# P4 of the second layer by a second Strassen level, with the sums of A22 added up by DMAs

## The chip, the core and the metric

The kernel runs on one core of a Trainium2 chip. The metric is the device time of one execution in microseconds; of several runs, the median. Five engines work side by side, each through its own list of instructions in order: TensorE (PE in the profile; its weight loads are PEld), VectorE (DVE), ScalarE (ACT), GpSimd (POOL) and SyncE (SP). SP and POOL also issue DMA transfers, which 16 DMA engines carry out. An instruction that waits for a semaphore holds up everything behind it in its engine's list.

## The reference

A light convolution, then two matrix products with a gate between them:

```python
# x: (8, 4096, 192), weight: (8, 7); softmax over the 7 taps of each of 8 heads
out = einsum('hk,bskhg->bshg', softmax(weight), windows_of_7(x))   # causal
x = out.reshape(32768, 192)
h = x @ w_in                      # 192 x 2048
g = h * clip(h + 3, 0, 6) / 6     # hardswish
return g @ w_out                  # 2048 x 192
```

## The kernel before

The 32768 tokens are taken in 32 blocks of 1024, and each of these as two halves of 512 (N). Block 0 is computed plainly, with `direct_chunk`; blocks 1 to 31 go through `first_layer` and then `second_layer`. The convolution of a later block runs beside them, as VectorE instructions over 128x1536 (L806, "taps").

**First layer.** 16 units, each 18 matmuls of 512 columns into one of four PSUM slots (two banks each). ScalarE computes the relu (L306) and VectorE the gate (L310), which frees the slot. Units 0 to 7 read `y_own` and give the tiles A11 and A22 of g, eight chunks of 128x512 each; units 8 to 15 read `y_other` and give A21 and A12. Beside them POOL forms the small sums of A11 (`small_sums` into `s1`, one pair of chunks after every second unit), then S3 = A11 - A21 (`g_sums(…, (3,), …)`, a pair of chunks after units 9, 11 and 13, the last pair on VectorE) and S1 = A21 + A22. The first two pairs of S1 are adding DMAs issued by POOL (L470, after units 9 and 11), the other two are VectorE adds.

**Second layer.** Written in Winograd's form of Strassen: seven products P1 to P7 of A and B tiles (and of the sums S and T) in place of eight (`prod` names operands of each). A product has 96 output rows, in three column groups q of 32; TensorE is split into four column strips of 32, and strips 0 to 2 compute the column groups of P4, P7, P2, P6, P3. Strip 3 computes P1 and P5, two of whose three column groups are done by one more Strassen level (`level_two`: products 1 to 7 of half size, `small`, on 256 tokens each; the third column group is plain). P1's surplus chunks go to strips 0 to 2.

The order is written out: `put(j, cost, fn)` appends a matmul to the list of strip j and moves its clock on, by 2 for 512 columns and by 1 for 256; one unit of this clock is called a step. `do(t, fn)` puts a copy, a sum or a DMA at time t. At the end all are sorted by time and issued, so a matmul that waits holds up all four strips. The clock sets the order alone; an engine starts an instruction when its own list and its waits allow it. The streams are 82 steps long. P1 to P7 are put together by matmul accumulation in PSUM banks a to e and x_, by ScalarE copies between banks and VectorE adds. `finish` adds and stores the last of a block in the first layer of the next one. SP issues `swap` (y_own to y_other), the loads of x and the stores.

Buffers that matter: `y_own` (two tiles, high and low part of the next block's y), `s1` (shares its tag with the result tiles, so it waits for their stores), A22, which the small sums of P5 (`s5`) overwrite once P4 has been computed.

Of the kernel before, what the change touches and what calls it, by code (L numbers as in the profile page):

```python
# [31 lines left out]
def kernel(  # L32
# [36 lines left out]
    ys = ctx.enter_context(tc.tile_pool(name="ys", bufs=1))  # L69
    ot = ctx.enter_context(tc.tile_pool(name="ot", bufs=1))  # L70
# [50 lines left out]
    y_own = [cst.tile([P, K3, N], F32, name=f"y{n}") for n in range(2)]  # L121
# [4 lines left out]
    w_s = cst.tile([P, 2, 4, NP // 2, QS], F32, name="w_s")  # L126

# [314 lines left out]

    def first_layer(i, jobs):
# [11 lines left out]
        count = 2 * NP  # L455
        for job in jobs.get(-1, ()):
            job()
        for n in range(count):
            unit(n)
            for job in jobs.get(n, ()):  # L460
                job()
# [4 lines left out]
            if n > NP and n % 2:  # L466
                pair = slice(n - NP - 1, n - NP + 1)
                g_sums(nc.gpsimd if n + 1 < count else nc.vector, (3,), range(NP)[pair], 2)
                if n + 3 < count:
                    nc.gpsimd.dma_start(out=S1[:, pair], in_=A22[:, pair], accum_op=ALU.add)  # L470
        for pair in (slice(NP - 2, NP), slice(NP - 4, NP - 2)):
            add(S1[:, pair], A21[:, pair], A22[:, pair])

# [19 lines left out]
    def small_weights(to, w):  # L493
# [5 lines left out]
        for o, p, q in ((t1, b12, b11), (t2, b22, t1), (t3, b22, b12), (t4, b21, t2)):  # L499
            nc.gpsimd.tensor_tensor(out=o, in0=p, in1=q, op=ALU.subtract)  # L500

    def second_layer(i, between):
        last = i + 1 == NB
        ours = [free_slots.pop(0) for _ in range(3)]
        d, e, b, x_, a, c = (psum[:, 2 * n + k] for n in ours for k in range(2))
        ends = [psum[:, 2 * free_slots[0] + k] for k in range(2)] if last else [b, b]
# [5 lines left out]
        B, C, V = (bank[rows(3)] for bank in (x_, d, b))  # L512
        A, E = e[rows(3)], a[rows(3)]
# [28 lines left out]
        def small(n, m_, out, start=False):  # L542

            x, w = prod[n]
            sums, ws = (s1[-1], w_s[:, 0]) if n == 1 else (s5, w_s[:, 1])
            x11, x12, x21, x22 = four_parts(x)
            z1, z2, z3, z4 = four_parts(sums)
# [3 lines left out]
            t1, t2, t3, t4 = (ws[:, k] for k in range(4))  # L551
# [4 lines left out]
            for u in range(NP // 2):  # L556
                put(3, 1, lambda u=u: matmul(
                    3, out[:, lo], wm[:, u], xm[:, u], start and u == 0
                ))
# [14 lines left out]

        for q in range(NQ):
            plain(q, d, 4, q, every, True)
            before = (1, 6, NP)[q]
            plain(q, c, 7, q, every[:before], True)
            plain(q, e, 1, 2, range(5 + q, 6 + q))
            do(clock[q], copy, out=e[rows(q + 1)] if q < 2 else p1[third], in_=e[rows(q)])  # L580
            plain(q, c, 7, q, every[before:])
            plain(q, a, 2, q, every[:6], True)
# [8 lines left out]
        def level_two(n, p, chunks, order):  # L591
# [25 lines left out]
            for step in order.split():  # L617
                if step[0] == "x":
                    fill(int(step[1]))
                elif step[0] in "lh":  # L620
# [326 lines left out]
```

## Time and profile before

| | |
|---|---|
| median of 3 runs | 2220.78 us (2220.66 to 2221.22) |
| the profiled execution | 2220.6 us, its span 2218.5 us |
| granted TensorE clock | 1.0 |
| TensorE busy | 2211.4 us, 100% of the span |
| VectorE busy | 1808.9 us, 82% |
| ScalarE busy | 935.8 us, 42% |
| GpSimd busy | 827.9 us, 37% |
| relu L306 of one unit | 1118 ns, 512 times |
| gate L310 of one unit | 1218 ns, 512 times |
| adding DMA g<-g, 512 KB | 62 times, 5.0 us from issue to landing |

In a line of a timeline stand the start in us from the beginning of the span, the duration in us, the engine, the line of the kernel, the operation, what it writes and reads, how many instructions are merged in it, and in brackets how long the engine had stood idle before it and what ended that. In a line of the chain in order of time stand start, length and what. A group's line has its busy time in us and the mean of one in ns. A matmul of fp32 data is two records in the profile.

### The profile page before, as it was taken

What the parts mean: (1) busy time and instruction counts of PE and PEld (TensorE: products, weight loads), DVE (VectorE), ACT (ScalarE), POOL (GpSimd) and SP (SyncE); (2) the same over time, 40 slices, a digit from 0 to 9 for tenths busy, and PEclk for the clock granted to TensorE, in tenths of its full rate; (3) what the DMA queues carried; (4) which work ended last, traced back from release to release, by engine and by line L of the source; (5) the groups of instructions that cost most, each with busy time, mean ns of one, the idle gap of its engine ahead of it and who ended that gap; (6) DMA issues with size and microseconds to landing.
All of it is one profiled execution on the core that took longest, in us unless ns stands there. A gap on an engine that the chain in (4) does not pass through costs nothing.

```text
span 2218.5 us, 49343 instructions
## 1 busy us (share of the span) xinstructions
PE 2211.4 (100%) x21598; PEld 1535.2 (69%) x21598; DVE 1808.9 (82%) x1588; ACT 935.8 (42%) x1172; POOL 827.9 (37%) x706
## 2 busy tenths in 40 slices
PE   9999999999999999999999999999999999999999
PEld 5567776677776677766777667776667776677766
DVE  8878788888888888888888888888888888888866
ACT  7434443344433444433444334443344433344433
POOL 4434442244422344323444224442244432344322
PEclk9999999999999999999999999999999999999999
DMA  7333323433223332243332333322433224333232
GB/s 165 65 71 69 66 37 67 77 63 77 35 58 78 70 70 49 44 77 70 70 62 40 68 74 66 77 35 59 77 68 73 43 49 77 70 70 57 40 59 34
DMA packets 249095, 142.91 MB, mean 64 GB/s; under 512 B 207120, under 2 KB 212240, under 8 KB 248880
## 3 DMA queue, kind: packets, MB, share of 16 engines
q1 hardware_dynamic: 230392, 105.86, 23.7%
q0 software_dynamic: 17248, 33.64, 8.8%
q8 instruction: 169, 2.77, 0.5%
q10 hardware_dynamic: 1240, 0.27, 0.1%
q14 instruction: 46, 0.38, 0.1%
HBM read 31.72 MB, written 25.17 MB: 26 GB/s over the span
## 4 chain that ended last, share of the span: by engine, by line
PE 99%; ACT 0%; DVE 0%; POOL 0%; DMA 0%; issue 0%; POOLq 0%; ACTq 0%; DVEq 0%
PE psum L528 50%; PE psum L432 47%; PE psum L321 2%; PE psum L730 0%; PE psum L738 0%; ACT g L306 0%; DMA y_other<-y 0%; POOL w_in L220 0%; ACT scale L196 0%; ACT sig L193 0%; ACT sig L199 0%; POOL sig L210 0%; ACT w_in L218 0%; DVE y L283 0%; POOLq L942 0%
## 5 line engine op out<-in xcount | busy, mean ns | idle before, releaser
L528 PE MATMUL psum<-g,w_out 128*32 128x512 f32 (+1 forms) x6712 | 967.4, 552 | 0.0
L306 ACT ACTIVATE g<-psum,half 128x1024 f32<-128x1024 f32 x512 | 572.3, 1118 | 494.0 <-PE psum L432 465.8
L310 DVE SCALAR_TENSOR_TENSOR g<-g,psum 128x1024 f32<-128x1024 f32 x512 | 618.8, 1218 | 195.1 <-ACT g L306 194.8
L491 POOL TENSOR_TENSOR s<-g 128x256 f32<-128x256 f32 x248 | 268.8, 1084 | 1252.5 <-DVE g L310 915.9
L528 PEld LDWEIGHTS psum<-g,w_out 128*32 128x32 f32 x6712 | 370.8, 110 | 246.9 <-issue 126.7
L432 PE MATMUL psum<-y,w_in 64*128 64x512 f32 x4608 | 534.8, 388 | 0.3
L432 PE MATMUL psum<-y_other,w_in 64*128 64x512 f32 x4608 | 529.0, 386 | 0.1
L432 PEld LDWEIGHTS psum<-y,w_in 64*128 64x128 f32 x4608 | 428.6, 184 | 121.3 <-issue 26.0
L432 PEld LDWEIGHTS psum<-y_other,w_in 64*128 64x128 f32 x4608 | 431.6, 184 | 91.1 <-DMA y_other<-y 0.5
L528 PE MATMUL psum<-s,w_out 128*32 128x512 f32 (+1 forms) x3272 | 465.4, 570 | 0.0
L806 DVE SCALAR_TENSOR_TENSOR y<-x,c_sb,y 128x1536 f32<-128x1536 f32 x186 | 334.8, 1800 | 2.1 <-ACT y L804 1.0
L380 POOL TENSOR_TENSOR s<-g 128x1024 f32<-128x1024 f32 x93 | 297.8, 3202 | 25.1 <-DVE g L310 25.1
L528 PE MATMUL psum<-g,w_s 128*32 128x256 f32 x1240 | 282.8, 379 | 0.0
L528 PEld LDWEIGHTS psum<-s,w_out 128*32 128x32 f32 x3272 | 153.7, 110 | 80.1 <-issue 48.3
L528 PEld LDWEIGHTS psum<-g,w_s 128*32 128x32 f32 x1240 | 136.4, 110 | 68.3
L380 DVE TENSOR_TENSOR s<-g 128x2048 f32<-128x2048 f32 (+1 forms) x93 | 177.1, 1931 | 1.1
L528 PE MATMUL psum<-s,w_s 128*32 128x256 f32 x744 | 170.7, 379 | 0.0
L491 DVE TENSOR_TENSOR g<-g 128x1024 f32<-128x1024 f32 x124 | 151.7, 1224 | 5.3
L380 DVE TENSOR_TENSOR g<-g 128x2048 f32<-128x2048 f32 x62 | 139.0, 2283 | 0.0
L400 DVE TENSOR_TENSOR p<-psum,p 32x256 f32<-32x256 f32 (+1 forms) x93 | 47.7, 513 | 96.5 <-PE psum L528 95.1
L400 DVE TENSOR_TENSOR results<-psum,results 32x256 f32<-32x256 f32 (+3 forms) x128 | 69.3, 541 | 50.8 <-issue 47.3
L525 ACT COPY psum<-psum 32x512 f32<-32x512 f32 x93 | 51.3, 551 | 135.4 <-PE psum L528 135.4
(88 smaller groups left out, 1089.1 us busy)
## 6 DMA issues: line engine op xcount, KB each, us to landing
y_other<-y SPq DMA_DIRECT2D x124, 384.0 KB, 4.9
g<-g POOLq DMA_DIRECT2D x62, 512.0 KB, 5.0
out_dram<-results SPq DMA_DIRECT2D x378, 64.0 KB, 2.0
x<-in_x_dram SPq DMA_DIRECT2D x53, 388.5 KB, 7.1
g<-in_moe_w_in_dram SPq DMA_DIRECT2D x16, 192.0 KB, 5.7
stage<-in_moe_w_out_dram SPq DMA_DIRECT2D x8, 384.0 KB, 5.7
x<-in_x_dram SPq DMA_DIRECT2D x7, 384.0 KB, 6.5
y_other<-y SPq DMA_DIRECT2D x12, 128.0 KB, 2.3
```

Source lines behind the costliest of these rows:

```text
L306: nc.scalar.activation(r6, h, ACT.Relu, bias=half[:], scale=1.0 / 6.0)
L310: nc.vector.scalar_tensor_tensor(out=g_, in0=g_, scalar=1.0, in1=h, op0=ALU.min, op1=ALU.mult)
L321: lambda p=p: nc.tensor.matmul(out=bank[j * QS : (j + 1) * QS, tokens], lhsT=w_out[:, p, w, cols], rhs=x[:, p, tokens], start=(first and p ...
L380: engine.tensor_tensor(out=o[:, r], in0=a[:, r], in1=b[:, r], op=op)
L400: nc.vector.tensor_tensor(out=out, in0=x, in1=y, op=op)
L432: nc.tensor.matmul(out=psum[:, 2 * slot + k], lhsT=r32(w_in_parts[wn][r, c, s]), rhs=r32(y_other[r, yn, s] if group else y_own[yn][r, s]), ...
L491: engine.tensor_tensor(out=o, in0=p, in1=q, op=op)
L525: streams[3].append((t - 0.5, lambda: fn(*args, **kw)))
L528: nc.tensor.matmul(out=out, lhsT=w, rhs=x, start=start, stop=True, tile_position=(0, j * QS), skip_group_check=True,)
L806: jobs.append(lambda k=k: nc.vector.scalar_tensor_tensor(out=y[:], in0=x[:, :, k : k + N], scalar=c_sb[:, k : k + 1], in1=y[:], op0=ALU.mu ...
```

## The change

P4 (A22 times T4) is no longer plain. Its column groups 0 and 1 are computed by the second Strassen level, as P1's and P5's are, but spread over strips 0, 1 and 2 (`small4`: products 1, 2 and 5 in strip 0, 6 and 3 in strip 1, 7 and 4 in strip 2). Its third column group is plain, its chunks spread over the three strips too (bank d, here `t4`). The results collect in a new tile `p4`. All streams are then 81 steps long; the order of P7, P2 and P1's surplus chunk around them is new, and P1 hands half a chunk more to strip 2.

The level needs four sums of quarters of A22. They are formed in the first layer: ScalarE writes seeds (copies of a quarter, by 1 or -1), and POOL issues adding DMAs onto them: `z13` twice, for half the chunks each (z1 = x21 + x22 and -z3 = x21 - x11, 512 KB a time), then z2 = z1 - x11 (512 KB), then z4 = z2 - x12 (512 KB). z2 and z4 lie in the buffers of `y_own`, so the next block's high and low part of y are split later (at 43.6 and 57.3 instead of 13 and 15) and swapped later (58 instead of 18). The weights' sums `w_s4` are formed once. S1's two DMAs become one of four chunks, after unit 11; POOL's list in a block is then: eight small sums, z13, eight small sums, z13, two pairs of S3, S1, z2, the third pair of S3, z4.

The banks of the second level change: the fourth slot (f, h) is used in every block, and P1 and P5 use other rows for their partial sums (A, B in f and h, C and E passed in). P1's and P5's orders of the seven products change. The sums s5 move to 15.5, 28.5 and 44, the fourth of them goes into `z`; S2 and the last S3 are formed in halves of four chunks.

```diff
             free_slots.append(slot)
         count = 2 * NP
+        x11, x12, x21, x22 = four_parts(A22)
+
+        def begin_sums():
+            z_early[:] = own_tiles("z")
+            seed(sums_a22()[1], x11, -1.0)
+
+        def seed(to, x, sign):
+            nc.scalar.mul(to, x, sign)
+
+        def onto(to, x):
+            nc.gpsimd.dma_start(out=to, in_=x, accum_op=ALU.add)
+
+
+        def z13(u0, u1):
+            onto(z[:, u0:u1].rearrange("p u c t -> p (u c) t"), A22[:, 2 * u0 : 2 * u1, halves[1]])
+
+        hu = NP // 4
+        s4_sums = {
+            hu + 1: [lambda: seed(z[:, :hu, 0], x11[:, :hu], -1.0)],
+            hu + 2: [lambda: seed(z[:, :hu, 1], x21[:, :hu], 1.0), lambda: z13(0, hu)],
+            NP - 1: [lambda: seed(z[:, hu:, 0], x11[:, hu:], -1.0)],
+            NP: [lambda: seed(z[:, hu:, 1], x21[:, hu:], 1.0), lambda: z13(hu, 2 * hu)],
+            NP + 1: [begin_sums],
+            NP + 2: [lambda: seed(sums_a22()[3], x12, -1.0)],
+        }
         for job in jobs.get(-1, ()):
             job()
         for n in range(count):
             unit(n)
             for job in jobs.get(n, ()):
+                job()
+            for job in s4_sums.get(n, ()):
                 job()
             if n == 1:
                 s1.append(ot.tile([P, NP, N], F32, name="s1", tag="shared")[:])
             if n > NP and n % 2:
                 pair = slice(n - NP - 1, n - NP + 1)
                 g_sums(nc.gpsimd if n + 1 < count else nc.vector, (3,), range(NP)[pair], 2)
-                if n + 3 < count:
-                    nc.gpsimd.dma_start(out=S1[:, pair], in_=A22[:, pair], accum_op=ALU.add)
+                if n == NP + 3:
+                    onto(S1[:, : NP // 2], A22[:, : NP // 2])
+                    onto(sums_a22()[1], z[:, :, 1])
         for pair in (slice(NP - 2, NP), slice(NP - 4, NP - 2)):
             add(S1[:, pair], A21[:, pair], A22[:, pair])
+        onto(sums_a22()[3], sums_a22()[1])
...
-        d, e, b, x_, a, c = (psum[:, 2 * n + k] for n in ours for k in range(2))
-        ends = [psum[:, 2 * free_slots[0] + k] for k in range(2)] if last else [b, b]
+        d, e, b, c, a, x_ = (psum[:, 2 * n + k] for n in ours for k in range(2))
+        ends = [psum[:, 2 * free_slots[0] + k] for k in range(2)]
...
-        B, C, V = (bank[rows(3)] for bank in (x_, d, b))
-        A, E = e[rows(3)], a[rows(3)]
...
+            if n == 4:
+                z1, z2, z3, z4 = sums_a22()
+                t1, t2, t3, t4, b22 = (w_s4[:, k] for k in range(5))
+            else:
+                sums, ws = (s1[-1], w_s[:, 0]) if n == 1 else (s5, w_s[:, 1])
+                z1, z2, z3, z4 = four_parts(sums)
+                if n == 5:
+                    z4 = z[:, :, 0]
+                t1, t2, t3, t4 = (ws[:, k] for k in range(4))
...
+        t4, (f, h) = d, ends
+        A4, B4, C4, E4 = x_[first, lo], x_[second, lo], x_[third, lo], f[first, lo]
+        A, B, V = f[fourth], h[fourth], b[fourth]
...
+        def plain_e(q):
+            plain(q, e, 1, 2, range(5 + q, 6 + q))
+            if q == 2:
+                plain_half(q, e, 1, 2, 4, 1)
+            do(clock[q], copy, out=e[rows(q + 1)] if q < 2 else p1[third], in_=e[rows(q)])
+
+        plain(0, t4, 4, 2, (0,), True)
+        plain_half(0, t4, 4, 2, 2, 0)
+        do(clock[0], copy, out=t4[second], in_=t4[first])
+        small4(0, 1, x_[first], True)
+        do(clock[0], copy, out=B4, in_=A4)
+        plain(0, c, 7, 0, every[:3], True)
+        plain_e(0)
+        plain(0, c, 7, 0, every[3:6])
+        small4(0, 2, x_[first])
+        do(clock[0], copy, out=p4[first, lo], in_=A4)
+        plain(0, c, 7, 0, every[6:])
+        small4(0, 5, f[first], True)
+        do(clock[0], copy, out=p4[second, lo], in_=E4)
+        plain(0, a, 2, 0, every[:6], True)
+
+        plain(1, c, 7, 1, every[:4], True)
+        plain_half(1, t4, 4, 2, 2, 1)
+        plain(1, t4, 4, 2, (1, 4, 6))
+        do(clock[1], copy, out=t4[third], in_=t4[second])
+        plain(1, c, 7, 1, every[4:6])
+        plain_e(1)
+        small4(1, 6, x_[second])
+        do(clock[1], copy, out=C4, in_=B4)
+        plain(1, c, 7, 1, every[6:])
+        plain(1, a, 2, 1, every[:5], True)
+        small4(1, 3, x_[second])
+        do(clock[1], add, p4[second, lo], B4, p4[second, lo])
+        plain(1, a, 2, 1, every[5:6])
+
+        plain(2, c, 7, 2, every[:4], True)
+        plain(2, a, 2, 2, every[:3], True)
+        plain(2, c, 7, 2, every[4:])
+        plain(2, t4, 4, 2, (3, 5, 7))
+        do(clock[2], copy, out=p4[third], in_=t4[third])
+        plain_e(2)
+        small4(2, 7, x_[third])
+        do(clock[2], add, p4[second, hi], C4, p4[second, lo])
+        plain(2, a, 2, 2, every[3:5])
+        small4(2, 4, x_[third])
+        do(clock[2], copy, out=p4[first, hi], in_=C4)
+        plain(2, a, 2, 2, every[5:6])
+
         for q in range(NQ):
-            plain(q, d, 4, q, every, True)
-            before = (1, 6, NP)[q]
-            plain(q, c, 7, q, every[:before], True)
-            plain(q, e, 1, 2, range(5 + q, 6 + q))
-            do(clock[q], copy, out=e[rows(q + 1)] if q < 2 else p1[third], in_=e[rows(q)])
-            plain(q, c, 7, q, every[before:])
-            plain(q, a, 2, q, every[:6], True)
+            assert clock[q] == 45
             plain(q, b, 6, q, every)
             plain(q, a, 2, q, every[6:])
             if last:
...
-        level_two(1, lambda: p1, range(5), "1 x5 6 5 2 7 3 4")
-        do(14, copy, out=e[first], in_=V)
+        level_two(1, lambda: p1, range(4), "x4 half 1 5 6 2 7 3 4", b[fourth], x_[fourth])
+        do(9, copy, out=e[first], in_=V)
         level_two(
             5, lambda: late["p5"], range(NP),
-            "1 l4 2 6 5 7 3 l2 4 l2 h8" if last else "1 x2 2 6 5 7 3 x1 4 x5",
+            "1 5 6 2 7 3 4 l8 h8" if last else "1 5 6 2 7 3 4 x8", x_[fourth], e[fourth],
         )
...
-        for t, n in ((16.2, 1), (16.2, 2), (30.5, 3), (34.5, 4)):
-            do(t, small_sums, s5, S1, (n,), nc.vector)
-        do(32, tiles)
-        do(34, lambda: copy(out=late["p7"], in_=c[m]))
-        do(38, copy, out=b[m], in_=p1[:])
-        do(38, g_sums, nc.vector, (2,), every, 4)
-        do(38, g_sums, nc.vector, (4,), every, 4)
-        do(62, lambda: add(late["u3"], b[m], late["p7"]))
-        do(62, lambda: add(late["p7"], late["u3"], d[m]))
-        do(62, lambda: store(i, late["p7"], 1, 0))
-        do(66, add, p1[:], a[m], p1[:])
-        do(66, lambda: store(i, p1, 0, 0))
+        def sum_s5(n):
+            if n < 4:
+                small_sums(s5, S1, (n,), nc.vector)
+            else:
+                s2 = four_parts(s5)[1]
+                add(z[:, :, 0], four_parts(S1)[1], s2, ALU.subtract)
+
+        for t, n in ((15.5, 1), (15.5, 3), (28.5, 2)):
+            do(t, sum_s5, n)
+        do(31, tiles)
+        do(37, copy, out=b[m], in_=p1[:])
+        do(37, g_sums, nc.vector, (2,), every[:4], 4)
+        do(43, g_sums, nc.vector, (2,), every[4:], 4)
+        do(44, sum_s5, 4)
+        do(44, g_sums, nc.vector, (4,), every[:4], 4)
+        do(53, lambda: copy(out=late["p7"], in_=c[m]))
+        do(61, lambda: add(late["u3"], b[m], late["p7"]))
+        do(61, g_sums, nc.vector, (4,), every[4:], 4)
+        do(65.5, lambda: add(late["p7"], late["u3"], p4[:]))
+        do(65.5, lambda: store(i, late["p7"], 1, 0))
+        do(65.5, add, p1[:], a[m], p1[:])
+        do(65.5, lambda: store(i, p1, 0, 0))
...
         if last:
-            do(74, end_lower)
+            do(73, end_lower)
         else:
-            do(82, lambda: copy(out=late["p5"][third], in_=V))
+            do(81, lambda: copy(out=late["p5"][third], in_=V))
...
         def split_high():
+            if z_early:
+                y_own[:] = own_tiles("y")
             high_of(y_own[HIGH][:], y[:])
...
+            small_weights(w_s4, T4, -1)
...
+        p4 = last.tile([DH, N], F32, name="p4")
+        z = last.tile([P, NP // 2, 2, TH], F32, name="z")
...
-                between = [(13, split_high), (15, split_rest), (18, swap_parts)]
+                between = [(43.6, split_high), (57.3, split_rest), (58, swap_parts)]
```

More of the change, by code (lines that the diff above doesn't have):

```diff
@@ L69 @@
     ys = ctx.enter_context(tc.tile_pool(name="ys", bufs=1))
+    yo = ctx.enter_context(tc.tile_pool(name="yo", bufs=1))
     ot = ctx.enter_context(tc.tile_pool(name="ot", bufs=1))
@@ L120, with own_tiles @@
     w_in_parts = [cst.tile([P, NP, K3, P], F32, name=f"w_in{n}") for n in range(3)]
-    y_own = [cst.tile([P, K3, N], F32, name=f"y{n}") for n in range(2)]
+    def own_tiles(name):
+        return [yo.tile([P, K3, N], F32, name=f"{name}{n}", tag=f"y{n}") for n in range(2)]
+    y_own, z_early = own_tiles("y"), []
     y_other = cst.tile([P, 2, K3, N], F32, name="y_other")
@@ L126 @@
     w_s = cst.tile([P, 2, 4, NP // 2, QS], F32, name="w_s")
+    w_s4 = cst.tile([P, 5, NP // 2, QS], F32, name="w_s4")
     w_in_bits = moe_w_in.bitcast(U32).rearrange("(p s) (c f w) -> c p s f w", s=K3, f=P, w=2)
@@ L440, in places, with sums_a22 @@
         return g4[:, c, 1:3] if group else g4[:, c, 0::3], psum[:, 2 * slot : 2 * slot + 2]
+    def sums_a22():
+        z2, z4 = (
+            part[:].rearrange("p s n -> p (s n)")[:, : NP * TH // 2]
+            .rearrange("p (u t) -> p u t", t=TH)
+            for part in z_early
+        )
+        return z[:, :, 1], z2, z[:, :, 0], z4
     def first_layer(i, jobs):
@@ L491, in small_sums, with small_weights @@
             engine.tensor_tensor(out=o, in0=p, in1=q, op=op)
-    def small_weights(to, w):
+    def small_weights(to, w, sign=1):
         b11, b12, b21, b22 = (
@@ L498, in small_weights @@
         t1, t2, t3, t4 = (to[:, n] for n in range(4))
-        for o, p, q in ((t1, b12, b11), (t2, b22, t1), (t3, b22, b12), (t4, b21, t2)):
+        third_sum = (t3, b22, b12) if sign > 0 else (t3, b12, b22)
+        for o, p, q in ((t1, b12, b11), (t2, b22, t1), third_sum, (t4, b21, t2)):
             nc.gpsimd.tensor_tensor(out=o, in0=p, in1=q, op=ALU.subtract)
+        if sign < 0:
+            nc.scalar.mul(to[:, 4], b22, -1.0)
     def second_layer(i, between):
@@ L540, in plain, with plain_half, small @@
                 ))
-        def small(n, m_, out, start=False):
+        def plain_half(j, bank, n, q, ch, t, start=False):
             x, w = prod[n]
-            sums, ws = (s1[-1], w_s[:, 0]) if n == 1 else (s5, w_s[:, 1])
+            put(j, 1, lambda: matmul(
+                j, bank[rows(j), halves[t]], w_out[:, ch, w, q * QS : (q + 1) * QS],
+                x[:, ch, halves[t]], start,
+            ))
+        def small(n, m_, out, start=False, j=3):
+            x, w = prod[n]
             x11, x12, x21, x22 = four_parts(x)
-            z1, z2, z3, z4 = four_parts(sums)
             b11, b12, b21, b22 = (
@@ L550, in small @@
             )
-            t1, t2, t3, t4 = (ws[:, k] for k in range(4))
+            if n == 4:
[7 more added lines that the diff above has]
+                t1, t2, t3, t4 = (ws[:, k] for k in range(4))
             xm, wm = {
@@ L556, in small @@
             for u in range(NP // 2):
-                put(3, 1, lambda u=u: matmul(
-                    3, out[:, lo], wm[:, u], xm[:, u], start and u == 0
+                put(j, 1, lambda u=u: matmul(
+                    j, out[:, lo], wm[:, u], xm[:, u], start and u == 0
                 ))
@@ new lines, in second_layer, with small4 @@
+        A4, B4, C4, E4 = x_[first, lo], x_[second, lo], x_[third, lo], f[first, lo]
+        A, B, V = f[fourth], h[fourth], b[fourth]
+        def small4(j, m_, out, start=False):
+            small(4, m_, out, start, j)
+        def plain_e(q):
[4 more added lines that the diff above has]
+        plain(0, t4, 4, 2, (0,), True)
@@ L589, in second_layer, with level_two @@
                 plain(q, b, 3, q, every)
-        def level_two(n, p, chunks, order):
+        def level_two(n, p, chunks, order, C, E):
             chunks, first_fill = list(chunks), [True]
@@ L619, in level_two @@
                     fill(int(step[1]))
+                elif step == "half":
+                    plain_half(3, b, n, 2, 4, 0)
                 elif step[0] in "lh":
```

## The prediction

> **What bounds the kernel now.** Three views were read, in this order. First the page: busy times and the chain that ended last.
>
> ```profile
> span 2218.5 us, 49343 instructions
> PE 2211.4 (100%) x21598; PEld 1535.2 (69%) x21598; DVE 1808.9 (82%) x1588; ACT 935.8 (42%) x1172; POOL 827.9 (37%) x706
> ...
> PE 99%; ACT 0%; DVE 0%; POOL 0%; DMA 0%; issue 0%; POOLq 0%; ACTq 0%; DVEq 0%
> PE psum L528 50%; PE psum L432 47%; PE psum L321 2%; PE psum L730 0%; PE psum L738 0%; ACT g L306 0%; DMA y_other<-y 0%; POOL w_in L220 0%; ACT scale L196 0%; ACT sig L193 0%; ACT sig L199 0%; POOL sig L210 0%; ACT w_in L218 0%; DVE y L283 0%; POOLq L942 0%
> ```
>
> TensorE is the chain: L432 is the first layer, L528 the second. Nothing else ends a wait that counts. Then the chain in order of time over one block, which is the block I use below:
>
> ```profile
> 914.73 32.87 PE psum L432 x288
> 947.60 35.47 PE psum L528 x216
> ```
>
> So a block is 32.87 + 35.47 = 68.34 us, and there are 31 of them with this second layer. Its streams are 82 steps long, so a step is 35.47 / 82 = 0.4326 us. TensorE waits for nobody, so a step less is a gain and any new wait is a loss at full price. Third, therefore, the timelines of the engines that must deliver on time. POOL in that block:
>
> ```profile
> 922.16 2.25 POOL L491 TENSOR_TENSOR s<-g 128x256 f32<-128x256 f32 x1 [40.88 <-DVE g L310]
> 924.49 0.73 POOL L491 TENSOR_TENSOR s<-s,g 128x256 f32<-128x256 f32 x1
> ...
> 936.34 0.73 POOL L491 TENSOR_TENSOR s<-g,s 128x256 f32<-128x256 f32 x1
> 937.85 3.93 POOL L380 TENSOR_TENSOR s<-g 128x1024 f32<-128x1024 f32 x1 [0.79 <-DVE g L310]
> 942.08 1.20 POOL L470 DMA_DIRECT2D g<-g  x1 [0.30 <-POOL s L380]
> 942.83 2.89 POOL L380 TENSOR_TENSOR s<-g 128x1024 f32<-128x1024 f32 x1
> 946.01 1.20 POOL L470 DMA_DIRECT2D g<-g  x1 [0.30 <-POOL s L380]
> 946.77 2.88 POOL L380 TENSOR_TENSOR s<-g 128x1024 f32<-128x1024 f32 x1
> ```
>
> POOL has almost no gap from its first sum to the end of the first layer: 0.79 us before 937.85 and twice 0.30. The ops of 2.25 and 3.93 us are ordinary ones that began while VectorE ran a convolution tap (the one below at 937.69). VectorE:
>
> ```profile
> 937.69 1.81 DVE L806 SCALAR_TENSOR_TENSOR y<-x,c_sb,y 128x1536 f32<-128x1536 f32 x1
> ...
> 960.82 0.43 DVE L400 TENSOR_TENSOR p<-psum,p 32x256 f32<-32x256 f32 x1 [3.02 <-PE psum L528]
> ...
> 968.53 4.49 DVE L380 TENSOR_TENSOR s<-g 128x2048 f32<-128x2048 f32 x2
> 974.56 1.13 DVE L400 TENSOR_TENSOR results<-psum,results 32x256 f32<-32x256 f32 x2 [1.54 <-issue]
> ...
> 978.97 3.63 DVE L806 SCALAR_TENSOR_TENSOR y<-x,c_sb,y 128x1536 f32<-128x1536 f32 x2
> 983.71 0.69 DVE L400 TENSOR_TENSOR results<-results 96x512 f32<-96x512 f32 x1 [1.11 <-ACT results L685]
> ```
>
> It has 3.02 and 1.54 us of slack in the second layer and starts the next block's work 983.71 - 983.07 = 0.64 us after the block ends. Last, the adding DMAs: their group on the page, and the DMA view of a stretch of 6 us (1078 to 1084) that holds the data of exactly one:
>
> ```profile
> g<-g POOLq DMA_DIRECT2D x62, 512.0 KB, 5.0
> ```
>
> ```profile
> q0 software_dynamic: 272, 0.52, 50.7%
> ```
>
> Of the 5.0 us from issue to landing, 0.507 x 6 = 3.04 us is data on all 16 engines, and 2.0 us is fixed.
>
> **The gain.** Every stream loses one step: 31 x 0.4326 = 13.4 us.
>
> **The sums of A22 (the term that decides).** Times t count from the block's first matmul. Before, the second adding DMA is issued at 946.01 - 914.73 = 31.28. After, POOL's list up to its S1 addition (now one of 1 MB, behind the second S3 pair) differs by:
> - two z13 issues in front, 1.20 each by the L470 row: +2.40;
> - the first S1 addition is gone from between the S3 pairs: -(0.30 + 1.20) = -1.50;
> - the idle 0.79 is used up: -0.79;
> - VectorE enters the block later. From step 43 of the second layer (18.6 us, plus 0.2 for drain and semaphore) its list is dense: three small adds at 0.43, the 4-chunk S2 half and two S3 halves at 2.25, the z sum 1.23, the low part of y 1.75, the 96x512 adds and transposes 0.68 + 0.68 + 0.71 + 0.69 + 0.71, two taps 3.63; together 18.1, so it ends at 36.9. The block now ends at 81 x 0.4326 = 35.04, so it is 1.9 us behind instead of 0.64. Gates 0 and 1 release POOL's first sum: +1.26.
>
> POOL meets the same three taps (after gates 1, 5 and 9) as before. Sum: 31.28 + 2.40 - 1.50 - 0.79 + 1.26 = 32.65. The z2 addition (512 KB) goes out right behind on the same queue. Three times 3.04 of data and 2.0 fixed: z2 lands at 32.65 + 11.1 = 43.8. TensorE wants it for product 6 of P4 in strip 1, at step 21: 32.87 + 9.08 = 41.95. It is 1.8 us late, and everything behind that matmul in TensorE's list waits, in all four strips.
>
> Bounds. Early end: VectorE is not late (0 for 1.26) and a z13 issue costs what plain POOL issues cost (x and the last stores, 0.62 to 0.66): issued at 30.3, landed at 41.4, no wait. Late end: issue time grows with the number of pieces (512 of 1 or 2 KB, against 256 of 2 KB): two z13 and S1 at 2.40, +3.6, and z2's 1 KB pieces take as long as 2 KB ones, +3.04: 8.4 us late. I take 1.8, since the L470 rows are this very operation, and the plain issues hardly vary with their pieces.
>
> The Trainium skill, "DMA: Bandwidth & Descriptors", section "Anatomy of one DMA", has a rule that speaks for the change: 2.0 us plus bytes over 436 GB/s. It makes 5.6 us of the 1.5 MB, so z2 would be there at 38.3. The trace disagrees: by that fit 512 KB take 3.2 us, and the adding DMA takes 5.0. By the rule the time would be the first rival's.
>
> **What else waits or moves.**
> - z4 is issued when z2 has landed: 43.9 + 5.0 = 48.9, wanted at step 39, 49.7 plus the 1.8 lost before: hidden.
> - POOL's third S3 pair now follows both issues: 35.05 to 37.45, or 38.7 behind one VectorE sum; P7 wants it at step 14, 38.9. Hidden, barely; 0 to 1 us, and what it costs z2's wait gets back.
> - In P1, product 4 (step 33) needs VectorE's add of product 7 (step 29), now behind the s5 sum keyed 28.5: 12.35 + 1.23 + 0.43 = 14.0 against 14.28. Nothing, at most 0.3.
> - Halved S2: first half from step 37 (16.2) to 18.5, wanted at 45 (19.5); the second by 21.5, wanted at 22.9. Hidden by 1 us.
> - ScalarE: four seeds near 0.6 us (96x512 copies: 0.58) and two near 1.1 (its 1024-element relu: 1.12) lie in the 0.92 us gaps between relus and push a relu by 0.3 at most; the eight copies of P4, 3.5 us, lie in a second layer where ScalarE mostly waits.
> - Gate 0 ends 1.26 later, near t = 7.5; unit 4 needs its slot at 8.2. Hidden by 0.7.
> - On SP the x load now stands ahead of the swaps, so it goes when the old x is free, near t = 25. It shares the DMA engines with z13's second half (issued near 26.4, landed near 33), which z2 needs only at its issue, 33.9. The swaps come after the low part of y, near 27.5 us into the second layer; group 1 wants them some 24 us later. Stores behind them still land before POOL's first sum is free by its gates.
> - w_s4: four POOL sums near 0.9 us and one ScalarE copy, once: 0 to 2 us. I take 0.
>
> Sum: 31 x (1.8 - 0.43) = +42 us. The profiled execution takes 2220.6 (span 2218.5 and 2.1 around it), the median of the runs is 2220.8, so nothing separates them: 2263.
>
> **Rivals.**
> 1. z2 is in time, faster: 2220.8 - 13.4 = 2207.4. It decides if S1's addition is issued before t = 30.8. For it: the early end. Against it: POOL's row without gaps.
> 2. z2 is 0.3 to 0.57 us late and eats the gain: 2216 to 2225.
> 3. POOL pays by pieces: 3.6 us later, late by 5.4: 2220.8 + 31 x 5.0 = 2375. Against it: the 32 KB stores in pieces of 128 B cost POOL 0.62, x in rows of 2 KB 0.66.
> 4. The step is not saved, because 256-column matmuls in several strips cost more: 2221 or, with z2 late, 2277. Against it stands the last block, which ends with 256 columns in all four strips and is no slower than the others:
>
> ```profile
> 2177.72 35.40 PE psum L528 x279
> ```
>
> **Chances.** z2 late by more than 0.6 us and less than 3.5: 0.54. Rival 1: 0.31. Rival 2: 0.05. Rival 3, and anything beyond 3.5 us late: 0.08. Rival 4: 0.02. 0.2% (4.4 us) is about what a measurement of this kernel tells from no change. So faster 0.31, same 0.06, slower 0.63. The likeliest case alone spans 2226 (0.6 late) to 2316 (3.5 late). With rival 1 the range is 2206 to 2310, leaving out about 0.1 above and little below.
>
> **What would show it.** In the chain, the second layer as two pieces with a wait on the DMA z<-z near 9 us after its start. Without it, L528 at 35.04 us per block means rival 1. In POOL's timeline the 1 MB addition near t = 32.65, issues of 1.2 us (2.4: rival 3). In VectorE's, the next block's first add 1.9 us after the second layer ends. The prediction is wrong if VectorE is not later, if a 1 MB addition takes less than twice 3.04 us of data, or if POOL gets through its sums with fewer taps in its way.

## The result: 22 us slower, and the profile after

The changed kernel takes 2243.1 us (median of 4 runs, 2242.97 to 2243.27) against 2221.0 us for the kernel before in the same session: a ratio of 1.0099, 95% interval 1.0081 to 1.0116. The prediction was 2263 in a range of 2206 to 2310. Its sign was right and its size was 20 us too large, but the way there was not the one it described: one cause weighed a fifth of what it was given, and two causes that it did not have made up most of the difference.

First the page of the changed kernel. L437 is now the first layer, L572 the second.

```profile
span 2241.4 us, 51884 instructions
...
PE 83%; DVE 10%; DMA 6%; POOL 1%; issue 0%; ACT 0%; SPq 0%; DVEq 0%; POOLq 0%; ACTq 0%
...
L437 PE MATMUL psum<-y,w_in 64*128 64x512 f32 x4608 | 548.9, 393 | 0.3
L437 PE MATMUL psum<-y_other,w_in 64*128 64x512 f32 x4608 | 530.1, 386 | 0.1
...
z<-g POOLq DMA_DIRECT2D x62, 512.0 KB, 5.7
g<-g POOLq DMA_DIRECT2D x31, 1024.0 KB, 8.2
z<-z POOLq DMA_DIRECT2D x62, 512.0 KB, 8.3
```

Before, 99% of the chain was TensorE. Now 10% runs through VectorE and 6% through DMAs. Less easy to see is the pair of matmul lines: the products that read `y_own` (`psum<-y`) take 548.9 us where they took 534.8 before, while those that read `y_other` are where they were (529.0 before). The change does not touch a single matmul of the first layer.

The chain in order of time, two blocks of it (start, length, what):

```profile
922.69 33.35 PE psum L437 x288
956.04 21.47 PE psum L572 x157
977.50 1.14 DVE z L405
978.64 2.20 DVE s L385
...
981.33 1.77 DVE y L423
...
983.58 0.70 DVE results L405
984.27 0.04 issue
984.32 7.07 PE psum L572 x64
991.39 31.33 PE psum L437 x270
1022.72 0.02 issue
1022.74 11.95 DMA z<-z
1034.69 0.04 issue
1034.74 10.34 PE psum L572 x97
```

Three things differ from the two lines of the kernel before. The first layer is 33.35 instead of 32.87 us. The second layer of the first block shown is cut at 984.32, 28.3 us after its start: TensorE was released there by VectorE, and behind that stands VectorE's whole list from 977.50 on. The second layer of the next block is cut at 1034.74 by the addition of z2. The waits of TensorE and its weight loads (total us, times, longest):

```profile
PEld psum L572 <- DVE results L405: 26.3, 60, 0.6
PEld psum L572 <- DMA z<-z: 9.8, 19, 1.0
...
PE psum L572 <- DMA z<-z: 2.0, 6, 0.5
```

These totals count the time since the engine's last instruction and so hold more than the loss. The loss itself is read from the lengths of the second layers. A block that does not wait for z2 takes 35.36 us, 0.32 more than the 35.04 that 81 steps make. That is the wait at 28.3. Blocks that wait for z2 take up to 36.40; the excess over 35.36, summed over 30 blocks, is 10.2 us.

So the wait on z2 that the prediction was about is there, at the place it was put (where nothing waits, in s1_half below, product 6 begins 9.05 us after the first matmul of the second layer; 9.08 was predicted), but in about every second block and 0.34 us long on average instead of 1.8. What VectorE does ahead of the other cut:

```profile
981.33 1.76 DVE L423 TENSOR_TENSOR y<-y,y 128x1536 fp32r<-128x1536 f32 x1
983.12 1.14 DVE L405 TENSOR_TENSOR results<-psum,results 32x256 f32<-32x256 f32 x2
984.18 2.28 DVE L385 TENSOR_TENSOR s<-g 128x2048 f32<-128x2048 f32 x1
...
992.60 0.68 DVE L405 TENSOR_TENSOR results<-results 96x512 f32<-96x512 f32 x1
```

The line at 983.12 holds two additions, a small one and u3 = bank b + P7 (`late["u3"]`), which ends at 984.26. P3 is accumulated into bank b from step 65 on, so TensorE may not write there until u3 has read it. In three_edits below, which does not wait there, P3 begins 27.95 us after the first matmul of the second layer. Here that first matmul starts at 955.97 (the chain counts from 956.04), so P3 would begin at 983.92 without a wait; it begins at 984.32. u3 stands behind the low part of y (L423), which the change moved from step 15 to step 57.3. In the kernel before, u3 ended at 975.69, 0.2 us before it was needed.

Three losses, then: `y_own`, u3, z2. Each was taken apart by itself.

### The profile page after: what moved, and what is told of

Read it like the earlier page. It is cut to its first block, busy times and chain, and to the rows that moved or that the text cites. A ratio compares the mean times of both kernels' runs of the same rounds, so it can differ in the third digit from the quotient of the medians.

```text
span 2241.4 us, 51884 instructions
## 1 busy us (share of the span) xinstructions
PE 2227.6 (99%) x22466; PEld 1531.3 (68%) x22466; DVE 1833.1 (82%) x1650; ACT 1163.6 (52%) x1607; POOL 900.7 (40%) x803
## 4 chain that ended last, share of the span: by engine, by line
PE 83%; DVE 10%; DMA 6%; POOL 1%; issue 0%; ACT 0%; SPq 0%; DVEq 0%; POOLq 0%; ACTq 0%
PE psum L437 45%; PE psum L572 35%; DMA z<-z 5%; DVE s L385 3%; DVE y L423 2%; DVE results L405 2%; PE psum L326 2%; DVE z L405 2%; POOL s L534 1%; PE psum L850 0%; POOL s L385 0%; DVE y L926 0%; DMA w_sb<-in_weight_dram 0%; DMA y_other<-y 0%; POOL z L480 0%
## 5 line engine op out<-in xcount | busy, mean ns | idle before, releaser
L572 PE MATMUL psum<-g,w_out 128*32 128x512 f32 (+1 forms) x6092 | 1051.2, 531 | 0.0
L572 PE MATMUL psum<-s,w_out 128*32 128x256 f32 (+1 forms) x3272 | 628.9, 571 | 2.9
L437 PE MATMUL psum<-y,w_in 64*128 64x512 f32 x4608 | 548.9, 393 | 0.3
L437 PE MATMUL psum<-y_other,w_in 64*128 64x512 f32 x4608 | 530.1, 386 | 0.1
L572 PEld LDWEIGHTS psum<-g,w_out 128*32 128x32 f32 x6092 | 421.7, 110 | 146.9 <-issue 44.0
L437 PEld LDWEIGHTS psum<-y,w_in 64*128 64x128 f32 x4608 | 428.0, 184 | 135.5 <-issue 26.7
L437 PEld LDWEIGHTS psum<-y_other,w_in 64*128 64x128 f32 x4608 | 431.7, 184 | 92.7 <-DMA y_other<-y 0.5
L572 PE MATMUL psum<-g,w_s 128*32 128x256 f32 x1488 | 322.3, 379 | 0.0
L572 PEld LDWEIGHTS psum<-s,w_out 128*32 128x32 f32 x3272 | 180.4, 110 | 168.6 <-issue 116.7
L534 DVE TENSOR_TENSOR g<-g 128x1024 f32<-128x1024 f32 x93 | 111.2, 1224 | 121.6 <-PE psum L572 121.6
L572 PE MATMUL psum<-z,w_s 128*32 128x256 f32 x992 | 201.8, 380 | 2.4 <-DMA z<-z 2.0
L572 PEld LDWEIGHTS psum<-g,w_s 128*32 128x32 f32 x1488 | 156.7, 110 | 39.8
L480 POOL DMA_DIRECT2D z<-z x62 | 83.4, 1345 | 233.5 <-ACT psum L718 81.0
L572 PE MATMUL psum<-s,w_s 128*32 128x256 f32 x744 | 170.7, 379 | 0.0
L569 ACT COPY psum<-psum 32x512 f32<-32x512 f32 (+1 forms) x217 | 106.3, 490 | 106.9 <-PE psum L572 103.1
L477 ACT ACTIVATE z<-g 128x512 f32<-128x512 f32 x186 | 143.2, 770 | 30.5 <-DVE g L315 30.4
```

The costliest lines, as they stand in the source:

```text
L437: nc.tensor.matmul(out=psum[:, 2 * slot + k], lhsT=r32(w_in_parts[wn][r, c, s]), rhs=r32(y_other[r, yn, s] if group else y_own[yn][r, s]), ...
L477: nc.scalar.mul(to, x, sign)
L480: nc.gpsimd.dma_start(out=to, in_=x, accum_op=ALU.add)
L534: engine.tensor_tensor(out=o, in0=p, in1=q, op=op)
L569: streams[3].append((t - 0.5, lambda: fn(*args, **kw)))
L572: nc.tensor.matmul(out=out, lhsT=w, rhs=x, start=start, stop=True, tile_position=(0, j * QS), skip_group_check=True,)
```

## The experiments

### 1. Why units 0 to 7 are slower

One theory was the traffic that is new beside those units (seeds, adding DMAs). The other was the place of `y_own` in SBUF: for z2 and z4 to share its buffers, the change took it out of the pool `cst` and gave it a pool of its own behind `ys`. The first three runs: the move alone, made in the kernel before; the changed kernel with `y_own` where x lay; and the changed kernel with `y_own` 32 bytes further on.

```diff
 # own_moved, from the kernel before
     ys = ctx.enter_context(tc.tile_pool(name="ys", bufs=1))
+    yo = ctx.enter_context(tc.tile_pool(name="yo", bufs=1))
-    y_own = [cst.tile([P, K3, N], F32, name=f"y{n}") for n in range(2)]
+    y_own = [yo.tile([P, K3, N], F32, name=f"y{n}") for n in range(2)]
 # own_first, from the changed kernel: yo opened ahead of xs, not behind ys
 # own_pad, from the changed kernel
+    yo.tile([P, 8], F32, name="pad")
     y_own, z_early = own_tiles("y"), []
```

> The kernel before with one edit: the two y_own tiles lie behind y in SBUF, as they do after the change (they lay among the constants). Nothing else of the change is made. Theory (the place of y_own slows units 0 to 7, which read it): units 0 to 7 take 2.10 us instead of 2.04 each, the first layer 33.34 instead of 32.87 us, so 31 x 0.47 = +14.6 us, about 2235.5. Rival (seeds and adding DMAs that run beside those units slow them): no change, 2221, first layer 32.87.

> The changed kernel with one edit: the pool of y_own is opened before those of x and y, so y_own lies where x lay. All instructions and their order are those of the changed kernel. Theory (placement): units 0 to 7 take 2.04 us, the first layer 32.87, 31 x 0.47 = 14.6 us less than 2243.1, if it is the relation to x and y that counts: 2228.5; a shorter first layer may leave z2 later against its use by part of the 0.47 and give some of it back. Rival (traffic): 2243, first layer 33.34.

> The changed kernel with 32 bytes per partition left free ahead of y_own: y_own then begins at 32 modulo 64, as it did in the kernel before, and not at 0 modulo 64. Theory in a narrower form (the alignment to 64 bytes of the rows that the matmul reads is what slows them): first layer 32.87 us, about 2228.5. If it is the place among the other tiles that counts: still 33.34 us, 2243. Rival (traffic): 2243 too.

Measured: own_moved 2236.1 us against 2220.8 (ratio 1.0068, 1.0052 to 1.0085), own_first 2242.8 (1.0099, 1.0084 to 1.0114), own_pad 2233.9 (1.0058, 1.0043 to 1.0073). In own_moved the first layer is:

```profile
L433 PE MATMUL psum<-y,w_in 64*128 64x512 f32 x4608 | 548.8, 393 | 0.3
L433 PE MATMUL psum<-y_other,w_in 64*128 64x512 f32 x4608 | 530.4, 387 | 0.1
```

So the move alone costs 15.3 us, without one instruction of the change, and traffic is out. That own_first is no faster says that being behind x and y is not it. In own_pad 32 bytes bring a unit from 2.10 to 2.06 us (2.04 before), so it is something fine about the address. Rows of `y_own` are 2048 bytes, and what the kernels shown so far differ in is where those rows begin against multiples of 2048 (the traces hold no addresses; these places follow from the sizes of the tiles and the order of the pools, each tile rounded up to 32 bytes): 160 bytes behind one in the kernel before, 64 ahead of one after the change, 576 ahead in own_moved, 160 ahead in own_first, 32 ahead in own_pad. Two runs crossed offset with place:

```diff
 # moved_160, from own_moved
+    yo.tile([P, 184], F32, name="pad")
     y_own = [yo.tile([P, K3, N], F32, name=f"y{n}") for n in range(2)]
 # low_576, from the kernel before
+    cst.tile([P, 328], F32, name="pad0")
     y_own = [cst.tile([P, K3, N], F32, name=f"y{n}") for n in range(2)]
+    cst.tile([P, 184], F32, name="pad1")
```

> The kernel before with y_own behind y in SBUF, as in own_moved, and 736 bytes per partition left free ahead of it, so that the rows of y_own begin 160 bytes behind a multiple of 2048, as in the kernel before, and not 576 bytes ahead of one. Theory (where the 2048-byte row that the matmul reads crosses a multiple of 2048 sets its rate): first layer 32.87 us, 2221. Rival (the part of SBUF in which y_own lies, high up beside x and y, sets it): 33.34 us, 2236, as in own_moved.

> The kernel before with y_own in its old place among the constants, but 1312 bytes per partition further on, so that its rows begin 576 bytes ahead of a multiple of 2048 as in own_moved; y_other keeps its 160 bytes behind one. Theory (offset of the row): units 0 to 7 at 2.10 us, first layer 33.34, 2236. Rival (part of SBUF): 32.87, 2221.

Measured: moved_160 2220.75 us (ratio 1.0, 0.9991 to 1.0009), units 2.04; low_576 2235.9 (1.0068, 1.0053 to 1.0083), units 0 to 7 2.10. The offset decides, the place does not. But a row that begins 128 behind a multiple of 2048 was slow too (three_edits, below), so what is good about 160? The weights of the first layer, `w_in0` to `w_in2`, begin 160 behind one as well, in all these kernels. The last run moved the weights:

```diff
 # weights_32, from the kernel before
+    cst.tile([P, 8], F32, name="pad0")
     w_in_parts = [cst.tile([P, NP, K3, P], F32, name=f"w_in{n}") for n in range(3)]
+    cst.tile([P, 504], F32, name="pad1")
     y_own = [cst.tile([P, K3, N], F32, name=f"y{n}") for n in range(2)]
+    cst.tile([P, 8], F32, name="pad2")
```

> The kernel before with the first layer's weights and y_other moved on by 32 bytes per partition against multiples of 2048 (from 160 to 192 behind one) and y_own still at 160. Three theories of what the rate of a matmul depends on. The difference between the offsets of weights and y: group 0 (y_own) 2.10 us a unit, group 1 (y_other, moved with the weights) 2.04. The offset of y's rows alone, of which only 160 has been fast so far: group 0 2.04, group 1 2.10. Both would give 2235; what tells them apart is the groups. That the rows of y begin at 0 modulo 64 in nearly all slow cases is a third: y_other then begins at 0 modulo 64, which gives the same as the second.

Measured: 2235.6 us (ratio 1.0066, 1.0052 to 1.0080), with

```profile
L435 PE MATMUL psum<-y,w_in 64*128 64x512 f32 x4608 | 548.5, 394 | 0.2
L435 PE MATMUL psum<-y_other,w_in 64*128 64x512 f32 x4608 | 529.9, 386 | 0.0
```

`y_own`, still at 160 but now against weights at 192, is slow; `y_other`, at 192 like the weights, is fast, although its rows begin at 0 modulo 64. So it is the offset of the moving rows against the weights that counts. All kernels in one table, with the places at which the tiles begin modulo 2048:

| kernel | weights | y_own | difference | unit 1 to 7, us |
|---|---|---|---|---|
| before, moved_160, best | 160 | 160 | 0 | 2.04 (best: unit 4's wait apart) |
| own_pad | 160 | 2016 | -192 | 2.06 |
| after, s1_half and others with its y_own | 160 | 1984 | -224 | 2.10 |
| own_first | 160 | 1888 | -320 | 2.10 |
| own_moved, low_576 | 160 | 1472 | -736 | 2.10 |
| three_edits | 160 | 128 | -32 | 2.10 |
| weights_32, y_own | 192 | 160 | -32 | 2.10 |
| weights_32, y_other | 192 | 192 | 0 | 2.04 |

Of the tiles' differences only zero has been seen to be free. For single matmuls the table says more. A matmul reads 128 columns of weights, 512 bytes per partition, and these pieces follow one another in the tile, so in the kernel before the weights of single matmuls begin 0, 512, 1024 or 1536 bytes apart from the rows, modulo 2048. Their pairs start 0.2266 or 0.2267 us apart all the same, so multiples of 512 are free too. Which other differences are free, whether the modulus is 512 or a divisor of it, and what in the chip causes it stays open. The Trainium skill, "TensorE: Matmul & The Clock Gate", section "Step-by-step: what each phase is for", says that TensorE reads the streamed operand and the weights through two independent ports, so that loading weights takes no read bandwidth from a matmul. By that the difference should not matter; 2.10 against 2.04 us in weights_32 says that it does.

### 2. The wait for u3

```diff
 # u3_first, from the changed kernel
-                between = [(43.6, split_high), (57.3, split_rest), (58, swap_parts)]
+                between = [(43.6, split_high), (61.5, split_rest), (62, swap_parts)]
```

In u3_first the first tap of the next convolution, at 60, overwrites y before its low part is taken, so that part is made from other numbers; VectorE's and TensorE's instructions are the same.

> The changed kernel with the low part of y split behind u3 and the last half of S3 (61.5 instead of 57.3; the swaps at 62 instead of 58). VectorE's work is the same, only its order is other. Theory (TensorE waits at step 65 for u3, which reads bank b before P3 may add to it, and u3 stands behind the low part of y): the wait of 0.3 to 0.4 us at 28.4 us after the start of the second layer goes, 31 x 0.35 = 11 us less; VectorE ends when it did, so against the shorter block z2's addition comes 0.35 us later, which costs up to 0.35 in every second block, 5 us. Together 2235 to 2238. Rival (the wait is on something else): 2243.

Measured: 2240.9 us (ratio 1.0090, 1.0075 to 1.0105), a gain of 2.2 us. The waits on `DVE results` are gone from the list and the shortest second layers are 35.04 us, so the wait was on u3. But most of the time came back as z2's:

```profile
PEld psum L572 <- DMA z<-z: 14.7, 23, 1.3
```

The mean second layer is 35.61 us instead of 35.70: of the 0.32 saved, 0.23 is spent again, waiting for z2. I had expected about half to be given back, not three quarters, and the reason was to be that VectorE's list would end when it did while the block got shorter. VectorE's list shows another one:

```profile
980.70 0.43 DVE L405 TENSOR_TENSOR results<-psum,results 32x256 f32<-32x256 f32 x1
982.37 1.15 DVE L405 TENSOR_TENSOR results<-psum,results 32x256 f32<-32x256 f32 x2 [1.24 <-PE psum L572]
...
997.88 2.34 DVE L315 SCALAR_TENSOR_TENSOR g<-g,psum 128x1024 f32<-128x1024 f32 x2
```

VectorE now stands idle for 1.24 us ahead of u3, where the low part of y used to fill the gap, and has the low part still to do behind it. Gate 0 of the next block starts 7.0 us after the block's start instead of 5.6, and POOL's first sum 1.4 us later. POOL makes up for most of that (its first two pairs of S3 take 5.6 us there, and 6.5 with a wait of 0.2 for a gate in the changed kernel), but S1's addition still goes out 0.4 us later, and z2 with it.

### 3. The wait for z2

Two ways to take it away: let TensorE want z2 later, or let z2 come earlier.

```diff
 # z2_later, from the changed kernel
-        small4(1, 6, x_[second])
-        do(clock[1], copy, out=C4, in_=B4)
         plain(1, c, 7, 1, every[6:])
+        small4(1, 6, x_[second])
+        do(clock[1], copy, out=C4, in_=B4)
 # z2_later_u3: this, u3_first, and
-  (60, lambda: conv[0]())
+  (62.5, lambda: conv[0]())
 # s1_half, from the changed kernel
-                    onto(S1[:, : NP // 2], A22[:, : NP // 2])
+                    onto(S1[:, : NP // 4], A22[:, : NP // 4])
-        for pair in (slice(NP - 2, NP), slice(NP - 4, NP - 2)):
+        for pair in (slice(NP - 2, NP), slice(NP - 4, NP - 2), slice(NP - 6, NP - 4)):
```

> The changed kernel with one edit: in strip 1 the two last chunks of P7 stand ahead of product 6 of P4, so TensorE wants z2 at step 25 instead of 21, 1.73 us later. Theory (the only waits on z2 are those of up to 1.1 us near 9.2 us after the start of the second layer): they all go, 10 us less, second layer 35.36 us in every block, 2233. Rival (the copy behind product 6 now has 2 steps, 0.87 us, before product 7 wants it, and is not done in time): a new wait of 0.1 to 0.5 us at step 31, 31 x 0.3 = 9 us given back, 2242.

> Both at once: z2 wanted at step 25, and the low part of y split behind u3 and the last half of S3 (at 61.5, swaps at 62; the first tap of the next convolution, which overwrites y, at 62.5 instead of 60). Theory (both waits are of their own, and what u3_first gave back was z2's wait alone): second layer 35.04 us in every block, 2243 - 10 - 10 = 2223. Rival (z2 is then 0.35 us later once more and waits at step 25 too, or VectorE's list puts a third wait in place): second layer above 35.2, 2228 or more.

> The changed kernel with one edit: S1's adding DMA covers two chunks (512 KB) instead of four, and VectorE adds the other two (one more add of 1.18 us at the end of the first layer, ahead of 3.2 us of VectorE idle time in the second). Theory (z2 queues behind S1's data, at 3.04 us for 512 KB, as the prediction had it, and only its size was wrong): the last packet of z2 comes 3.0 us earlier, at 4.7 to 6.5 us after the start of the second layer instead of 7.7 to 9.5, all waits on z2 go and none takes their place, second layer 35.36 us in every block, 10 us less, 2233. Rival (z2's end is set by something else than the data queued ahead, the instruction fetch that falls into it or the 1 KB pieces): waits on z2 stay in every second block, 2238 or more.

Measured: z2_later 2251.2 us (ratio 1.0137, 1.0121 to 1.0154), slower than the change itself. z2 is no longer waited for, but every second layer is 35.96 us:

```profile
PEld psum L572 <- DVE results L405: 26.1, 60, 0.6
PEld psum L572 <- ACT p L569: 16.1, 31, 0.5
```

The new wait of 0.60 us stands at 10.8 us, step 25:

```profile
971.16 0.36 ACT L569 COPY p<-psum 32x256 f32<-32x256 f32 x1 [0.78 <-PE psum L572]
...
971.57 0.11 PEld L572 LDWEIGHTS psum<-z,w_s 128*32 128x32 f32 x1 [0.52 <-ACT p L569]
```

There product 6 of P4 begins in strip 1, into bank x_, and it waits for ScalarE's copy of product 2's sum out of strip 0's rows of the same bank, which begins at that very step. In the changed kernel both products run from step 21 to 25, and the copy follows both. So the kind of wait was the one that the rival had named, but the copy was another one. The weight load waits for ScalarE's semaphore and starts 0.05 us after that copy has ended. The copy and the product touch different rows of the bank and exchange no data; that the program orders accesses by whole banks would explain the wait, but no run shows it. The Trainium skill, "PSUM — Partial Sum Buffer", section "PSUM bank collisions raise a hardware error", says that different groups of 32 partitions of one bank may be accessed at the same time; by that, strip 1's product would not have to wait for strip 0's copy. No run here tried it without the wait.

z2_later_u3, 2243.2 us (1.0101, 1.0086 to 1.0116), has second layers of 35.67 us (one of 35.76), the new wait alone. Against z2_later it gains 8.0 us (31 x 0.29 = 9.0 by the second layers): where z2 is not in the way, taking u3's wait away is worth that, and not 2.2.

s1_half takes 2232.6 us (1.0053, 1.0037 to 1.0068), 10.5 less than the change, as expected. All second layers are 35.35 or 35.36, and TensorE's list of waits has no DMA of z left. In the packets of the trace z2's data begin 1.4 us after the start of the second layer instead of 4.5 to 4.9 and end at 4.6 to 5.7 instead of 7.9 to 9.5: z2 had queued behind S1's data. VectorE's extra add cost nothing.

### 4. All three taken away

```diff
 # three_edits: s1_half, the order of z2_later_u3 without z2_later's, and yo opened first of all pools
+    yo = ctx.enter_context(tc.tile_pool(name="yo", bufs=1))
     cst = ctx.enter_context(tc.tile_pool(name="cst", bufs=1))
 # best: the same, but w_sb, g and w_in_parts in a pool cst0 ahead of yo
+    cst0 = ctx.enter_context(tc.tile_pool(name="cst0", bufs=1))
+    yo = ctx.enter_context(tc.tile_pool(name="yo", bufs=1))
     cst = ctx.enter_context(tc.tile_pool(name="cst", bufs=1))
```

> Three edits of the changed kernel at once: S1's DMA of two chunks as in s1_half; the low part of y behind u3 and the last half of S3 as in z2_later_u3; and y_own at the very front of SBUF, its rows 128 bytes behind a multiple of 2048 (they lay 64 bytes ahead of one). Theory (these three are all that the change lost against its 13.4 us of saved steps): first layer 32.87, second 35.04 us, a block 67.91 against 68.34 before; 31 x 0.43 = 13.4 us less than the kernel before, plus about 1.4 us at start and end as in the changed kernel: 2207 to 2209. Rival (something else still waits, or the three overlap): above 2212.

> three_edits with y_own at the very address that it has in the kernel before (its pool opened behind the first layer's weights, its rows 160 bytes behind a multiple of 2048) instead of at the front of SBUF. Theory (what three_edits had left was y_own alone, whose new place was no good one): first layer 32.87, second 35.04 us in every block; 2222.7 - 31 x 0.47 = 2208.1, or 13.4 less than the kernel before by the steps alone, 2207.5. Rival (with units 0 to 7 faster again, z2 or u3 is late against a shorter block): second layers above 35.1, 2212 or more.

Measured: three_edits 2222.7 us (ratio 1.0008, 0.9999 to 1.0017). All second layers are 35.04, but the first layers are still 33.33 or a little more: the front of SBUF was no better place, which led to weights_32. best takes 2213.3 us (ratio 0.9965, 0.9952 to 0.9979), 7.6 us less than the kernel before. That is 5 to 6 us short of what was expected. Its chain and its waits:

```profile
911.79 33.03 PE psum L438 x288
944.82 35.04 PE psum L573 x253
```

```profile
PEld psum L438 <- DVE g L316: 8.1, 29, 0.7
```

The second layer is at its 81 steps. The first is 33.03 and not 32.87: unit 4 takes 2.19 instead of 2.04 us, since it waits for the PSUM slot that gate 0 frees. Gate 0 is late for the reason seen in u3_first, VectorE's idle time ahead of u3:

```profile
901.58 0.43 DVE L406 TENSOR_TENSOR results<-psum,results 32x256 f32<-32x256 f32 x1
903.23 1.15 DVE L406 TENSOR_TENSOR results<-psum,results 32x256 f32<-32x256 f32 x2 [1.23 <-PE psum L573]
...
918.74 2.34 DVE L316 SCALAR_TENSOR_TENSOR g<-g,psum 128x1024 f32<-128x1024 f32 x2
```

It idles 1.23 us at 903.23 and starts gate 0 at 918.74, 6.95 us after the block's start (911.79). In the changed kernel gate 0 starts 5.57 after it (996.96 against 991.39). Over the 30 later blocks the first layers are 5.4 us longer than in the kernel before, which is the shortfall.

## Why the prediction was right in sign and wrong in its working

The budget, in us against the kernel before:

| | worth | from |
|---|---|---|
| one step less | -13.4 | 31 x 0.4326; 35.04 us in three_edits and best |
| y_own's offset against the weights | +15.3 | own_moved alone |
| wait for z2 | +10.5 | the change less s1_half |
| wait for u3 | +9.9 | 31 x 0.32; three_edits and s1_half differ by 9.9 |
| sum | +22.3 | measured: 22.1 |

The worths hold beside one another and not each by itself: in u3_first, where u3 does not wait, z2 costs 17.0 us (30 second layers against 35.04) and not 10.5.

- **The gain** was right: every step of it is there once nothing waits. Rival 4 (the step not saved) is out.
- **The sums of A22.** That z2 queues behind S1 and where TensorE waits for it was right; the term was sized 1.8 us a block and measured 0.34. The step that failed is the issue time of S1's addition, 32.65 in the prediction and 30.4 to 30.6 in the trace. That is even ahead of the 30.8 which the prediction had named as the mark of rival 1 (z2 in time). POOL's timeline shows why:

```profile
930.68 2.25 POOL L534 TENSOR_TENSOR s<-g 128x256 f32<-128x256 f32 x1 [32.93 <-DVE g L315]
...
937.31 0.75 POOL L534 TENSOR_TENSOR s<-g,s 128x256 f32<-128x256 f32 x1
938.00 1.28 POOL L480 DMA_DIRECT2D z<-g  x1
938.82 1.47 POOL L534 TENSOR_TENSOR s<-g 128x256 f32<-128x256 f32 x1
...
945.36 1.26 POOL L480 DMA_DIRECT2D z<-g  x1
946.30 3.91 POOL L385 TENSOR_TENSOR s<-g 128x1024 f32<-128x1024 f32 x1
...
953.08 1.29 POOL L480 DMA_DIRECT2D g<-g  x1 [0.30 <-POOL s L385]
953.87 1.80 POOL L480 DMA_DIRECT2D z<-z  x1
```

Against the block's start, 922.69: POOL's first sum begins at 7.99 instead of 7.43 before, +0.56 where +1.26 was predicted. VectorE's first add of the next block comes 1.21 us after the second layer ends (992.60 against 991.39), not 1.9, in part because the block did not shrink as foreseen (the u3 wait itself gave VectorE 0.32). An issue of 1.28 us delays the next sum by about 0.6 (938.82 less 937.31 is 1.51; the same step took 0.89 before), not by 1.20, because the next sum starts before its record ends. The old pair of lines at 942.08 and 942.83 showed that too: 0.75 from the one start to the next. I took the duration of the record for the delay. The tap that had stretched a small sum to 2.25 us now falls largely on that issue (VectorE runs it from 937.82 to 939.68), and the sum behind it takes 1.47: 0.8 less. That comes near the last of the three signs by which the prediction said it would be wrong, a tap less in POOL's way. The second z13 cost 0.1 instead of 0.4 and the S3 pairs gave back 1.4 instead of 1.5. Together 0.70 + 0.58 + 0.80 + 0.30 - 0.12 = 2.26, the whole difference. The other part of the term, 11.1 us from the issue of S1's addition to the landing of z2, holds in some blocks: 11.1 us in the first block shown (z2 lands 8.2 us after the start of the second layer, 0.8 before it is wanted), but 12.7 in the second (it lands at 10.0). Over all blocks it is 11.1 to 11.9, except in the 14 blocks in which a packet of the instruction queue falls into z2's transfer: there it is 12.2 to 12.8, and these blocks wait 0.3 to 1.0 us each. The longer first layer, for its part, let TensorE want z2 0.47 us later than predicted. So by the predicted 11.1 z2 would not have been late at all; it is late where its transfer takes a microsecond longer, which the prediction did not have.
- **Rival 3** (issue time grows with the pieces) is out for z13 and S1: 1.28, 1.26 and 1.29 us with twice the pieces of the 1.20 us before; z2's own issue, right behind S1's, took 1.80.
- **VectorE.** The prediction saw that its list is dense from step 43 on and used that only to find when it ends. It did not ask who waits for each entry on the way. u3 is one of them: it has to end before step 65, it had 0.2 us to spare before, and the low part of y was moved ahead of it. This is the step that was left out, and the lines for it were there: 974.56 + 1.13 and the first matmul of P3.
- **The first layer** was taken as unchanged, 32.87. Nothing in the trace of before speaks of the offset, as both groups had the same one as the weights; the diff, though, said that y_own moves.
- **Hidden, as predicted:** z4, the third S3 pair (done 2.1 us into the second layer, wanted at step 14), the halves of S2, the seeds, gate 0. The last was called hidden by 0.7 us, and it is the next to appear when VectorE gets later by 1.4 (best).

So the number came near because the two causes that were missed, 25 us, replaced a good half of the 45 us by which z2 was oversized. The sign, too, is luck: with z2's waits alone, 10.5 to 17.0 us against the 13.4 saved, the kernel would have come out at about 2218 to 2224 by this budget, the prediction's rival 2, to which it had given 0.05.

## What to carry to other kernels

When an edit moves work within a dense engine list, go through the list entry by entry and ask what each one releases and by when; the end of the list is only one of the deadlines. Taking one wait away can bring the next one closer, so its gain alone says little of its weight: u3's paid 2.2 us alone and 9.9 beside s1_half's edit. And when a tile gets another address, compare the mean duration of the instructions that read it, even if the code that reads it is untouched.

## What the runs showed of the hardware

- A matmul pair of 512 columns (fp32r, 64 rows each, two row groups side by side) takes 0.2267 us when moving rows and weights begin at the same offset modulo 512, and 0.2333 at most other differences tried (0.2289 at one), 3% more: 15 us in weights_32 for weights moved by 32 bytes.
- The record of a DMA issue on POOL (1.2 to 1.3 us) overlaps the next instruction: that one starts 0.75 to 0.95 us after it. From 256 to 512 pieces (before; z13 and S1) the record grew from 1.20 to between 1.26 and 1.29 us.
- In 14 blocks of the changed kernel, every second one, a packet of the instruction queue (16 KB, about 0.95 us) falls 7.0 to 8.1 us after the start of the second layer, into z2's transfer, and in those blocks z2's last packet comes at 9.0 to 9.5 instead of 7.9 to 9.0 us. It fits that one of the 16 DMA engines is held up by it, but no run set the two apart.
